# Attention of two batch pairs and a dense block: the second pair interleaved with the first pair's dense layers, row sums as a value column, the Sinkhorn matrix built on chip, s and b applied at the output

The kernel runs on one core of one Trainium2 chip. The metric is the device time of an execution in microseconds; unless said otherwise a time is the median.

## The reference, cut to what matters

```python
# attention: q, k, v are (4, 8, 768, 64), sort_net is (4, 8, 8, 8); 8 blocks of 96 rows
P = sort_net
for _ in range(5):
    P = exp(P - max(P, -1))
    P = P / (sum(P, -1) + 1e-9)
    P = P / (sum(P, -2) + 1e-9)
k_sorted = einsum('bhij,bhjcd->bhicd', P, k_blocks)      # v the same
scores = q_block @ k_sorted_block.T / 8                  # only block i with block i
attn = softmax(scores) @ v_sorted_block
x = attn as (3072 tokens, 512)
# dense block: 512 -> 2048 -> 512
h = x @ w_in
out = (s * relu(h)**2 + b) @ w_out                       # s, b are scalars
```

## The kernel before: the parts that matter

Cuts are marked with `...`. Everything is bf16 on TensorE. A scheduler orders the instructions of each engine by its own model of time, so the order of the source is not the order on the engine.

```python
pd_dram = dramp.tile([NG, 128, 128], BF)                 # zeroed in DRAM first
...                                                      # loads: k, q, v of both pairs, then w_in, w_out
...                                                      # Sinkhorn on sn[32, 8, 8], five rounds
for g in range(NG):                                      # block-diagonal matrix by way of DRAM
    for e in range(2):
        nc.sync.dma_start(out=dst, in_=pT[g * GBH + e * 8: g * GBH + e * 8 + 8])
for g in range(NG):
    nc.sync.dma_start(out=pdg[g], in_=pd_dram[g])
...                                                      # transforms of q, k, v of BOTH pairs
for n in range(L):                                       # up to 5 blocks of 96 tokens
    nc.tensor.matmul(out=pv[0:64, cs], lhsT=VS[:, :, gi_e], rhs=at_e[:, cs], start=True, stop=True)
    nc.tensor.matmul(out=pv[64:128, cs], lhsT=VS[:, :, gi_o], rhs=at_o[:, cs], start=True, stop=True)
    nc.tensor.matmul(out=sm[0:64, cs], lhsT=ones96, rhs=at_e[:, cs], start=True, stop=True)
    nc.tensor.matmul(out=sm[64:128, cs], lhsT=ones96, rhs=at_o[:, cs], start=True, stop=True)
nc.vector.reciprocal(out=smr[:, :W], in_=sm[:, :W])      # row sum repeated over 64 rows of the head
nc.vector.scalar_tensor_tensor(out=XT[:, hp, tok0:tok0 + W], in0=pv[:, :W], scalar=sqrt_s,
                               in1=smr[:, :W], op0=ALU.mult, op1=ALU.mult)
...
# dense block after all attention, 512 tokens at a time
...                                                      # 64 matmuls hps, relu on ACT, square on DVE
for f in range(NF):
    nc.tensor.matmul(out=ops_, lhsT=gt[:, f, m * 128:(m + 1) * 128], rhs=wo[:, f, :],
                     start=(f == 0), stop=False)
nc.tensor.matmul(out=ops_, lhsT=ones_row, rhs=bcs, start=False, stop=True)      # the bias
nc.vector.tensor_copy(out=ot, in_=ops_)
```

The softmax here doesn't subtract the row's maximum and nothing guards it: scores larger than these inputs give would overflow.

## Time and profile before

| | before |
|---|---|
| median, range of 4 runs | 368.1 us, 367.5 to 368.8 |
| profiled span | 366.6 us |
| PE, DVE, ACT, POOL busy | 288.7, 174.0, 120.2, 6.3 us |
| first dense matmul starts | 186.9 us |
| last dense matmul ends | 362.5 us |

The two last lines are from the chain in order of time. The span falls into a front of 187 us, in which loads, DMA waits, transforms and attention follow one another, and a dense part of 176 us in which PE is full. The prediction below shows the lines.

PE is TensorE, DVE VectorE, ACT ScalarE, POOL GpSimd, and PEld TensorE's loads of weights. The granted clock is the share of TensorE's full clock that the profile records. PSUM is the memory that matmuls write to, and to evacuate is to copy a result from there to SBUF. The chain is the work that ended last, followed back from the end of the run.

### The profile page before, as it was taken

The numbers are of one execution on the slowest core, as the hardware profiler recorded it, in microseconds if no ns is written. First come the engines' busy times: TensorE is split into PE (matmuls) and PEld (weight loads), VectorE is DVE, ScalarE is ACT, GpSimd is POOL, SyncE is SP. The second block draws the span as 40 slices with busy tenths as digits, with TensorE's granted clock in tenths as the row PEclk, the third lists the DMA queues.
The fourth block names the chain that finished last, engine by engine and source line by source line (L and its number), as shares of the span: only waits on it lengthen the run. The fifth ranks groups of instructions, "written<-read, shape, count | busy, mean of one in ns | idle before, by whom it ended". The sixth has DMA issues, their size and how long they took to land.

```text
span 366.6 us, 5743 instructions
## 1 busy us (share of the span) xinstructions
PE 288.7 (79%) x2472; PEld 169.9 (46%) x2472; DVE 174.0 (47%) x240; ACT 120.2 (33%) x225; POOL 6.3 (2%) x18
## 2 busy tenths in 40 slices
PE   0070258998666896666499999999999999999995
PEld 0050247987555785555234444444434444434442
DVE  0581250039999819999934124224314414413411
ACT  3100007794323562323036026107206404503600
POOL 6000000000000000000000000000000000000000
PEclk9999999566555555555599999999999999999999
DMA  7999999600000000000000110010010020011011
GB/s 129 217 216 217 215 205 206 107 2 3 2 2 0 2 0 2 0 2 2 1 0 2 57 57 2 29 72 14 30 57 29 3 80 34 2 57 57 2 57 57
DMA packets 8010, 20.42 MB, mean 56 GB/s; under 512 B 1586, under 2 KB 3634, under 8 KB 7218
## 3 DMA queue, kind: packets, MB, share of 16 engines
q0 software_dynamic: 3456, 13.63, 18.6%
q1 hardware_dynamic: 4530, 6.44, 4.9%
q8 instruction: 19, 0.31, 0.3%
q14 instruction: 5, 0.04, 0.0%
HBM read 27.34 MB, written 6.36 MB: 92 GB/s over the span
## 4 chain that ended last, share of the span: by engine, by line
PE 59%; DVE 22%; DMA 12%; ACT 2%; issue 2%; SPq 1%; ACTq 0%
PE hps L257 23%; DVE smr L228 18%; PE ps L174 6%; DMA pd_dram<-pT 5%; DMA pdg<-pd_dram 4%; DMA sn<-in_sort_net_dram 2%; DVE XT L229 2%; PE ps L159 2%; ACT ks L165 2%; PE cs_ps L245 1%; PE ops__3663 L266 1%; PE ops__3642 L266 1%; PE ops__3621 L266 1%; PE ops__3450 L266 1%; PE ops__3429 L266 1%
## 5 line engine op out<-in xcount | busy, mean ns | idle before, releaser
L228 DVE RECIPROCAL smr<-sm 128x480 f32<-128x480 f32 (+1 forms) x32 | 79.5, 2525 | 36.9 <-PE sm L224 36.9
L261 ACT ACTIVATE rt<-hps 128x512 bf16<-128x512 f32 x96 | 57.3, 597 | 113.0 <-PE hps L257 113.0
L257 PE MATMUL hps<-XT,wi 128*128 128x512 bf16 x384 | 83.9, 379 | 0.0
L262 DVE TENSOR_TENSOR gt<-rt 128x512 bf16<-128x512 bf16 x96 | 40.8, 425 | 44.8 <-ACT rt L261 44.8
L257 PEld LDWEIGHTS <-wi 128*128 128x128 bf16 x384 | 37.1, 98 | 45.5 <-issue 1.6
L266 PEld LDWEIGHTS <-gt 128*128 128x128 bf16 x384 | 36.1, 98 | 45.1 <-issue 4.1
L159 PE MATMUL ps<-ident,qb 128*64 128x64 bf16 x384 | 14.5, 241 | 36.5 <-DMA qb<-in_q_dram 34.3
L209 ACT ACTIVATE at_o<-sc_o 96x480 bf16<-96x480 f32 (+1 forms) x32 | 15.6, 487 | 54.6 <-PE pv L218 24.2
L159 PEld LDWEIGHTS <-qb 128*64 128x64 bf16 x384 | 12.1, 153 | 38.8 <-DMA qb<-in_q_dram 34.5
L222 PE MATMUL sm<-at_e,ones 96*64 96x96 bf16 x128 | 21.6, 273 | 9.0 <-DVE smr L228 8.7
L220 PE MATMUL pv<-at_o,vs 96*64 96x96 bf16 x128 | 22.7, 300 | 6.2 <-ACT at_o L209 6.1
L218 PE MATMUL pv<-at_e,vs 96*64 96x96 bf16 x128 | 22.7, 305 | 4.2 <-DVE XT L229 3.5
L165 ACT CAST ks<-ps 128x512 bf16<-128x512 f32 x24 | 12.9, 589 | 37.9 <-PE ps L159 37.8
L201 PE MATMUL sc_o<-qt,ks 64*96 64x96 bf16 x128 | 16.9, 270 | 9.3 <-ACT at_o L209 9.3
L218 PEld LDWEIGHTS <-vs 96*64 96x64 bf16 x128 | 19.3, 199 | 10.0 <-issue 8.8
L174 PE MATMUL ps<-pdg,vb 128*96 128x128 bf16 x128 | 23.6, 347 | 0.4 <-ACT ks L165 0.2
L174 PEld LDWEIGHTS <-vb 128*96 128x96 bf16 x128 | 22.6, 254 | 0.9
L167 DVE CAST qt<-ps 128x512 bf16<-128x512 f32 x24 | 15.5, 687 | 15.6 <-PE ps L159 14.3
L220 PEld LDWEIGHTS <-vs 96*64 96x64 bf16 x128 | 18.7, 203 | 4.3 <-issue 4.2
L176 ACT CAST vs<-ps 96x512 bf16<-96x512 f32 x32 | 18.5, 581 | 5.9 <-PE ps L174 4.5
L224 PE MATMUL sm<-at_o,ones 96*64 96x96 bf16 x128 | 20.2, 276 | 0.0
L201 PEld LDWEIGHTS <-ks 64*96 64x96 bf16 x128 | 12.3, 174 | 12.5 <-issue 10.4
(111 smaller groups left out, 252.4 us busy)
## 6 DMA issues: line engine op xcount, KB each, us to landing
out_dram<-ot SPq DMA_DIRECT2D x24, 256.0 KB, 2.0
kb<-in_k_dram POOLq DMA_DIRECT2D x2, 1536.0 KB, 21.4
qb<-in_q_dram POOLq DMA_DIRECT2D x2, 1536.0 KB, 28.2
vb<-in_v_dram POOLq DMA_DIRECT2D x2, 1536.0 KB, 35.1
wi<-in_moe_w_in_dram POOLq DMA_DIRECT2D x1, 2048.0 KB, 55.2
wo<-in_moe_w_out_dram POOLq DMA_DIRECT2D x1, 2048.0 KB, 64.6
sn<-in_sort_net_dram SPq DMA_DIRECT2D x4, 2.0 KB
pd_dram<-zero SPq DMA_DIRECT2D x2, 32.0 KB, 19.3
```

The source lines that it names most:

```text
L159: nc.tensor.matmul(out=ps[e * 64:(e + 1) * 64, t, :], lhsT=src_t[:, c0 + t, :], rhs=mov[:, e * 64:(e + 1) * 64], start=True, stop=True)
L165: nc.scalar.copy(out=dstt[:, :, c0:c0 + CK], in_=pst)
L174: nc.tensor.matmul(out=ps[:, t, :], lhsT=Vb[:, :, d0 + t], rhs=pdg[g], start=True, stop=True)
L201: nc.tensor.matmul(out=sc_o[:, n * BLK:(n + 1) * BLK], lhsT=KS[64:128, q_idx * NB + i, :], rhs=QT[64:128, q_idx * NB + i, :], start=True, ...
L218: nc.tensor.matmul(out=pv[0:64, cs], lhsT=VS[:, :, gi_e], rhs=at_e[:, cs], start=True, stop=True)
L220: nc.tensor.matmul(out=pv[64:128, cs], lhsT=VS[:, :, gi_o], rhs=at_o[:, cs], start=True, stop=True)
L222: nc.tensor.matmul(out=sm[0:64, cs], lhsT=ones96, rhs=at_e[:, cs], start=True, stop=True)
L228: nc.vector.reciprocal(out=smr[:, :W], in_=sm[:, :W])
L257: nc.tensor.matmul(out=hps, lhsT=wi[:, hp, f * 128:(f + 1) * 128], rhs=XT[:, hp, t0:t0 + TG], start=(hp == 0), stop=(hp == NHP - 1))
L261: nc.scalar.activation(out=rt, in_=hps, func=AF.Relu)
L262: nc.vector.tensor_tensor(out=gt[:, f, :], in0=rt, in1=rt, op=ALU.mult)
L266: nc.tensor.matmul(out=ops_, lhsT=gt[:, f, m * 128:(m + 1) * 128], rhs=wo[:, f, :], start=(f == 0), stop=False)
```

## The change

It has five parts. (1) The Sinkhorn matrix is made on chip: a matmul with a 0/1 matrix spreads the rows of `sn` over partitions, and DVE masks them into block-diagonal form. (2) Loads, transforms and attention of the second batch pair become small pieces, called from slots between the dense matmuls of the first pair. (3) Two columns of ones stand beside the 64 value columns, so that the row sum comes out of the value matmul, one per token, and the reciprocal is taken of 8 numbers. For that the product is turned (tokens on partitions), and PE transposes it back. (4) s and b are applied in the copy of the output; the column sum of w_out comes from Pool and one fp32 matmul. (5) Tiles have 384 tokens, and PSUM is shared by all stages in double banks.

```diff
-    nc.sync.dma_start(out=dst, in_=pT[...])             # and back
+    nc.tensor.matmul(out=pe[:, 0:NB * NB], lhsT=emat[:, g * 128:(g + 1) * 128], rhs=sn..., ...)
+    ...                                                 # eight small DVE operations make pd
-    VSg.append(trs.tile([BLK, D, 128], BF, ...))
+    G.vs = trp.tile([BLK, 128, VW], BF, ...)            # VW = 66
+    nc.gpsimd.memset(G.vs[:, :, D:VW], 1.0)
-    ...                                                 # pv with VS stationary, sm with ones96
-    nc.vector.reciprocal(out=smr[:, :W], in_=sm[:, :W])
+    nc.tensor.matmul(out=pv[0:m, e, n * VW:(n + 1) * VW],
+                     lhsT=atf[:, c0:c0 + m], rhs=G.vs[:, e * 64 + g0 + n, :], ...)
+    nc.vector.reciprocal(out=rec, in_=pvv[:, :, :, D])  # 96 x 8
+    nc.vector.tensor_tensor(out=x..., in0=pvv[:, :, :, 0:D], in1=rec..., op=ALU.mult)
+    nc.tensor.transpose(out=tr..., in_=x..., identity=ident[0:BLK, 0:BLK])
...
+    for p in attention(G0, b2, half): p()               # first pair alone
+    nc.gpsimd.tensor_tensor(out=csum, in0=csum, in1=wo[:, f, :], op=ALU.add)   # 15 adds
+    nc.tensor.matmul(out=bps, lhsT=onesf, rhs=csum, start=True, stop=True)
+    nc.vector.tensor_scalar(out=bias, in0=bps, scalar1=b_bc, ...)
+    raws.append(load_raw(1)); G1, queue = transforms(1); queue += attention(G1, b2, half)
+    ffn1(0, nothing)
+    for t in range(NT):
+        if t + 1 < NT: ...; ffn1(t + 1, slot)           # slot() runs queued pieces
+        ffn2(t, slot)
-    nc.tensor.matmul(out=ops_, lhsT=ones_row, rhs=bcs, start=False, stop=True)
-    nc.vector.tensor_copy(out=ot, in_=ops_)
+    nc.vector.scalar_tensor_tensor(out=ot, in0=ops, scalar=s_bc, in1=bias, op0=ALU.mult, op1=ALU.add)
```

## The prediction

> **What bounds the kernel now.** I read the page's slices first, then the chain that ended last, then the groups by shape, then the stretches. The slices show four phases of 9.2 us slices: loading (to slice 7), transforms, attention on DVE (slices 8 to 19), and a dense stretch with PE at nine tenths.
>
> ```profile
> PE   0070258998666896666499999999999999999995
> DVE  0581250039999819999934124224314414413411
> PEclk9999999566555555555599999999999999999999
> GB/s 129 217 216 217 215 205 206 107 2 3 2 2 0 2 0 2 0 2 2 1 0 2 57 57 2 29 72 14 30 57 29 3 80 34 2 57 57 2 57 57
> ...
> PE 59%; DVE 22%; DMA 12%; ACT 2%; issue 2%; SPq 1%; ACTq 0%
> ```
>
> The chain says that no single engine bounds it: DMA holds the start, DVE the attention, PE the end. In the middle PE is half idle and its granted clock is about half. The chain in order of time gives the two DMA waits and the dense rhythm:
>
> ```profile
> 21.02 20.05 DMA pd_dram<-pT
> 41.13 13.93 DMA pdg<-pd_dram
> ...
> 115.06 4.96 DVE smr L228 x2
> ...
> 186.86 13.92 PE hps L257 x64
> 200.78 3.45 PE ops__2535 L266 x16
> 204.55 3.56 PE ops__2556 L266 x16
> 208.42 3.56 PE ops__2577 L266 x16
> ```
>
> The Sinkhorn matrix is ready at 21 us but goes through DRAM and is back at 55 us, queued behind the bulk loads. Two DVE reciprocals take 4.96 us and the next pair starts 5.84 us later (109.22, 115.06). One dense matmul of 512 columns takes 13.92/64 = 217.5 ns; an output tile starts every 3.87 us, although its 16 matmuls need 3.48, so the seventeenth, the bias matmul, costs 0.39.
>
> The stretches, whose columns are stretch, us, then busy us of PE, PEld, DVE, ACT, POOL, the clock, the DMA share and GB/s, show who is full in attention and in the dense part:
>
> ```profile
> 134.00:182.00 48.00, 29.07 (x372) 23.99 (x373) 46.34 (x32) 13.46 (x32) 0.00 (x0) 0.50 0.00 1
> ...
> 187.00:363.00 176.00, 175.78 (x792) 75.25 (x790) 57.56 (x121) 57.31 (x96) 0.00 (x0) 1.00 0.09 35
> ```
>
> DVE is 97% busy in the first, with clock 0.50; in the second PE is full, and DVE and ACT have two thirds free. These durations are used below:
>
> ```profile
> L228 DVE RECIPROCAL smr<-sm 128x480 f32<-128x480 f32 x16 | 50.4, 3150 | 36.9 <-PE sm L224 36.9
> L229 DVE SCALAR_TENSOR_TENSOR XT<-pv,sqrt_s,smr 128x480 bf16<-128x480 f32 x16 | 9.9, 620 | 0.0
> L167 DVE CAST qt<-ps 128x512 bf16<-128x512 f32 x24 | 15.5, 687 | 15.6 <-PE ps L159 14.3
> L209 ACT ACTIVATE at_o<-sc_o 96x480 bf16<-96x480 f32 x16 | 9.1, 568 | 11.7 <-PE sc_o L201 11.7
> ...
> 60.24 0.93 PE L159 MATMUL ps<-pdg,kb 128*64 128x64 bf16 x32 [0.18 <-ACT ks L165]
> 62.22 1.49 PEld L174 LDWEIGHTS <-vb 128*96 128x96 bf16 x8
> 123.01 2.82 PEld L174 LDWEIGHTS <-vb 128*96 128x96 bf16 x16
> ```
>
> The last three are from the timeline: a q or k transform matmul costs 0.93/32 = 29 ns, and a v transform, whose weights are read with a stride, 1.49/8 = 186 ns at full clock and 2.82/16 = 176 ns at half clock. It is its weight load that sets it, not the clock.
>
> **What the Trainium skill says.** "VectorE: DVE Perf Modes", the walkthrough of the pipeline, says that a reciprocal is an iterative division with a repeat count of 8. The trace agrees in kind: 480 and 288 elements take 3150 and 1900 ns, 6.5 ns each, where 512 plain copies take 692 ns. "TensorE: Matmul & The Clock Gate", Back-to-back issue gap, gives N/2.4 + 2.5 ns: 215.8 ns at 512 against 217.5 here. Its Part 1 says that an idle PE falls to half clock; the attention stretch shows 0.50. "GPSIMD Engine Reference", 3.1 Elementwise, gives 4497 ns for an add of 2048 fp32 elements; the trace before has no such operation, so this stays an estimate: 512 elements in about 1.15 us.
>
> **Part by part.**
>
> *Sinkhorn on chip.* The matrix load is now the first DMA, ahead of the bulk loads. In the trace before, s, sent first, was there within 3 us, so Sinkhorn starts at about 3.5 us instead of 11.6. Five rounds take 1.76 us each (11.65 to 20.4), plus a maximum and a subtraction: done at 13. The expansion by a small matmul and eight DVE operations of some 0.25 us ends at about 16 us, where before it was 55. This removes both DMA waits, 34 us of the chain.
>
> *Loads.* Only q, k, v of the first pair precede the weights. Before, 13.63 MB took from 3.7 to 70.2 us, 0.205 MB/us. Now 4.72 MB land by 25 us, wi by 36, wo (8.9 MB in all) by about 46. The second pair's loads come later, beside PE work.
>
> *Transforms of the first pair.* The instruction order puts the expansion matmul after 22 q matmuls, so PE stops until 14 us. Then 170 q and 192 k at 29 to 33 ns, 11.5 us, and 64 v at 0.18, 11.6 us: done at about 38. Evacuation by DVE (1024 elements, 1.22 us by the slope of the 512 copies) and ACT (1.02) in turn is 0.6 us a piece against 0.93 or 1.45 on PE, so hidden.
>
> *Attention.* The row sum as a value column turns 32 large reciprocals (80.8 us) into 32 of 8 elements (191 ns in Sinkhorn), and drops 256 row-sum matmuls. Per head pair and half batch DVE has 0.2 + 0.7 = 0.9 us, ACT one exponential of 768 columns, 0.80 us (slope 0.83 ns from 400 and 563), PE 8 score matmuls at 40 ns and 8 value matmuls at 60 to 100 ns, 0.8 to 1.1 us. With three double buffers, each held about 1.6 us, two per step, a step takes 1.1 to 1.3 us; four steps and the transposes (16 on PE, a copy of 1536 columns of 1.5 us) make a tile of 5.5 us. Before, one step over eight blocks took 5.84 us; two halves now take about 2.5.
>
> *The bias.* The 16 column-sum matmuls (5.3 us) and 24 bias matmuls (24 x 0.39 = 9.4 us) go away. In their place Pool adds 16 slices of wo: 15 adds at 1.15 = 17 us, with five DMA issues of 0.6 us among them, all after wo lands at 46. The one matmul that uses the sum stands in PE's order right after the first scores of the second tile, and waits for Pool. PE gets there at about 38 + 6 = 44 us; the sum is there at 46 + 17 + 3 = 66. PE works in order, so **22 us are lost here**, which the author probably did not intend. Then three tiles remain, 16.5 us: the dense part starts at about 84 us, against 187 before.
>
> *Dense part.* Tiles of 384 tokens: 512 first-layer matmuls at 384/2.4 + 4.2 = 164 ns, 84 us; 384 second-layer ones at 217.5, 83.5 us. Interleaved on the same PE: 384 transforms at 29 (11 us), 64 v at 180 (11.5), 16 steps at 0.8 (13), 64 transposes at 60 (4): 39.5 us. Some 70 changes between kinds of matmul at about 0.08 us, a guess, add 6. Together 213 us. DVE has 64 squarings of 768 columns at 0.56 (36), 24 output operations at 0.7 (17), evacuations 13 and attention 15, 81 us; ACT 64 x 0.80, evacuations 13 and exponentials 13, 77 us. Both are far below 213, so PE sets it.
>
> *Sum.* 84 + 213 = 297; after the last matmul 366.6 - 362.5 = 4.1 us of copy and DMA stay; the measured time is 1.6 above the profiled span (368.2, 366.6). This makes **302.7**; I round to 300, since my PE costs for attention lean high.
>
> **The rivals.**
> 1. *Pool is quick, or wo lands earlier.* With adds of 0.5 us the sum is ready at 57 us, the stall is 13 us, and the time about 290; with no stall at all 279. For it: Pool's small operations in the trace take 0.2 to 0.28 us for 128 columns. Against it: two inputs, fp32, and the skill's figure. If an add takes 2 us the stall is 35 us, and the time 315.
> 2. *Interleaving stalls PE.* All of hps, scores, values, transposes and transforms share three double buffers, and DVE and ACT serve them in order. A late evacuation then stops dense matmuls too, and a PE that pauses may fall to half clock, as in the attention before. At 0.25 us lost at each of 70 changes, 315 us. Against it: ACT and DVE would be under 40% busy, and a buffer comes round only after two other pieces, some 2.5 us of PE work.
> 3. *The second pair's loads come late.* Their buffers are the first pair's, and they are issued from between the Pool adds, from about 52 us, so 4.72 MB need until about 80. The first q piece stands behind 72 first-layer matmuls, about 84 + 12 = 96 us, v 20 us later. I expect no wait; if Pool takes 2 us an add, v is issued at 80 and still in time.
> 4. *Nothing gained,* because the dense part just grows by what it takes in. It grows by 37 us (176 to 213), yet 103 us vanish in front of it; all but impossible.
>
> **Range and chances.** The uncertain terms are the Pool sum (12 us either way), attention tiles (5), the interleaved work and its changes (10); combined about 16. Range 282 to 317. Even the worst corners of the rivals together, about 335, are 9% faster than 368.2.
>
> **What would show it right or wrong.** Pool should be busy from about 46 to 66 us, and the wait list should show the bias matmul waiting for the last Pool add about 20 us. No large reciprocal remains; the exponentials of 768 columns show 0.80 us. The clock should be 1.0 from the first dense tile to the end. PE's busy share from there should be over 95%. A PE gap inside the dense part, released by an evacuation or by the load of v, would prove rival 2 or 3; a short or missing wait of the bias matmul proves rival 1. The prediction fails most if the interleaved transforms cost PE much more than 29 ns in that company.

## The result, and the profile after

The changed kernel takes **297.6 us** (296.9 to 297.9, 4 runs) against 368.1. The ratio is 0.807, 95% interval 0.806 to 0.809. Here and below ratio and interval are from fast runs; the ratio is not quite that of the medians quoted.

The slices of the changed kernel's page (7.4 us each), and its chain's shares:

```profile
PE   0474982005899999999999999999999999999994
DVE  4763442003473455433533463434354255324221
POOL 8100003993000000000000000000000000000000
PEclk9997555555555999999999999999999999999999
...
PE 71%; ACT 3%; issue 2%; DVE 1%; ACTq 0%
```

The longest wait of PE, from the list of waits (us in total, times, longest):

```profile
PE bps L330 <- POOL csum L328: 22.9, 1, 22.9
```

From 69.5 us to the end the chain is PE almost alone; DVE has gone from 22% to 1%. The shares sum to 77% because the chain, as the profile follows it back, begins with the bias matmul at 69.5 us. What held that matmul is in the list of waits: the Pool adds, and PE's zeros in slices 7 and 8 lie under Pool's nines (third row).

The stretches of the changed kernel, with the columns explained in the prediction: the wait, the rest of the first pair's attention, the dense part.

```profile
46.70:69.50 22.80, 0.00 (x0) 0.00 (x0) 0.00 (x0) 0.81 (x1) 19.89 (x20) 0.50 0.59 112
71.60:91.00 19.40, 16.95 (x234) 14.32 (x232) 13.16 (x27) 10.10 (x12) 0.33 (x1) 0.50 0.45 96
91.00:292.00 201.00, 199.12 (x1652) 114.58 (x1666) 78.95 (x133) 77.41 (x93) 0.00 (x0) 0.99 0.09 31
```

Attention is no longer full on DVE (13.2 of 19.4 us where it had 46.3 of 48.0), and PE is full for 201 us of dense work with everything interleaved. The groups that answer to those of before, by shape:

```profile
L296 DVE TENSOR_TENSOR gt<-rt 128x768 bf16<-128x768 bf16 x64 | 35.6, 556 | 49.6 <-ACT rt L295 49.5
L233 ACT ACTIVATE at<-sc 96x768 bf16<-96x768 f32 x32 | 25.5, 805 | 59.6 <-PE sc L229 59.4
L254 DVE TENSOR_TENSOR x<-pv,rec 96x512 bf16<-96x512 f32 x32 | 22.0, 686 | 1.1
L328 POOL TENSOR_TENSOR csum<-csum,wo 128x512 f32<-128x512 f32 x14 | 16.2, 1156 | 0.8
L253 DVE RECIPROCAL rec<-pv 96x8 f32<-96x8 f32 x32 | 6.4, 201 | 11.2 <-PE pv L248 10.2
```

80.8 us of reciprocals (50.4 for the 16 of 480 elements, 30.4 for the 16 of 288) have become 6.4. The timeline of PE (start, us, what, the number of instructions) gives the marks of the front and the rates in the dense part:

```profile
12.52 1.08 PE L147 MATMUL pe<-sn,emat 32*128 32x64 f32 x4 [2.29 <-DVE identf L101]
28.83 10.75 PE L206 MATMUL tv<-pd,vb 128*96 128x128 bf16 x64 [1.16 <-DMA vb<-in_v_dram]
69.53 2.07 PE L330 MATMUL bps<-csum,onesf 128*128 128x512 f32 x2 [22.91 <-POOL csum L328]
104.69 0.69 PE L196 MATMUL tp<-ident,qb 128*64 128x64 bf16 x32
105.32 1.47 PE L290 MATMUL hps<-xt,wi 128*128 128x384 bf16 x8
161.14 0.38 PE L229 MATMUL sc<-qt,ks 64*96 64x96 bf16 x8
161.45 3.63 PE L304 MATMUL ops<-wo,gt 128*128 128x512 bf16 x15
```

The on-chip matrix is started at 12.5 us, where before its way through DRAM ended at 55. Between dense matmuls 32 transform matmuls take 105.32 - 104.69 = 0.63 us, 20 ns each, and eight score matmuls 0.31 us.

So the dense part starts at 91.0 us instead of 186.9 (95.9 us gained), and lasts to 291.9, which is 200.9 us instead of 175.6 (25.3 lost to the interleaved work): 70.6 us in all, as measured.

### The profile page after: what moved, and what is told of

It is laid out like the page before. It is cut to its first block, busy times and chain, and to the rows that moved or that the text cites. A ratio compares the mean times of both kernels' runs of the same rounds, so it can differ in the third digit from the quotient of the medians.

```text
span 295.9 us, 5457 instructions
## 1 busy us (share of the span) xinstructions
PE 245.7 (83%) x2421; PEld 155.4 (53%) x2438; DVE 117.1 (40%) x220; ACT 104.1 (35%) x126; POOL 27.9 (9%) x42
## 4 chain that ended last, share of the span: by engine, by line
PE 71%; ACT 3%; issue 2%; DVE 1%; ACTq 0%
PE hps L290 28%; PE ops L304 28%; PE tv L206 3%; PE pv L248 3%; PE sc L229 3%; PE tr L265 2%; PE tp L196 2%; ACT at L233 2%; ACT rt L295 1%; PE bps L330 1%; DVE ks L171 0%; DVE ot L307 0%; DVE gt L296 0%; ACT xt L173 0%; ACTq L233 0%
## 5 line engine op out<-in xcount | busy, mean ns | idle before, releaser
L290 PE MATMUL hps<-xt,wi 128*128 128x384 bf16 x512 | 91.5, 330 | 0.5 <-ACT rt L295 0.5
L304 PE MATMUL ops<-wo,gt 128*128 128x512 bf16 x367 | 83.7, 379 | 1.1 <-issue 0.5
L295 ACT ACTIVATE rt<-hps 128x768 bf16<-128x768 f32 x64 | 51.8, 811 | 44.6 <-PE hps L290 42.5
L304 PEld LDWEIGHTS <-gt 128*128 128x128 bf16 x384 | 36.4, 98 | 41.8
L296 DVE TENSOR_TENSOR gt<-rt 128x768 bf16<-128x768 bf16 x64 | 35.6, 556 | 49.6 <-ACT rt L295 49.5
L233 ACT ACTIVATE at<-sc 96x768 bf16<-96x768 f32 x32 | 25.5, 805 | 59.6 <-PE sc L229 59.4
L307 DVE SCALAR_TENSOR_TENSOR ot<-ops,s_bc,bias 128x512 f32<-128x512 f32 x24 | 18.0, 751 | 59.1 <-PE ops L304 59.1
L206 PE MATMUL tv<-pd,vb 128*96 128x128 bf16 x128 | 21.7, 343 | 1.2 <-DMA vb<-in_v_dram 1.2
L206 PEld LDWEIGHTS <-vb 128*96 128x96 bf16 x128 | 21.7, 256 | 1.7 <-DMA vb<-in_v_dram 1.3
L254 DVE TENSOR_TENSOR x<-pv,rec 96x512 bf16<-96x512 f32 x32 | 22.0, 686 | 1.1
L330 PE MATMUL bps<-csum,onesf 128*128 128x512 f32 x2 | 2.1, 1140 | 22.9 <-POOL csum L328 22.9
L248 PE MATMUL pv<-vs,at 96*128 96x66 bf16 (+1 forms) x256 | 17.3, 221 | 2.7 <-ACT at L233 2.6
L328 POOL TENSOR_TENSOR csum<-csum,wo 128x512 f32<-128x512 f32 x14 | 16.2, 1156 | 0.8
L171 DVE CAST vs<-tv 96x1024 bf16<-96x1024 f32 x8 | 9.8, 1221 | 15.9 <-PE tv L206 15.9
L229 PE MATMUL sc<-qt,ks 64*96 64x96 bf16 x256 | 14.7, 249 | 1.1 <-ACT xt L173 0.7
```

The source lines that it names most:

```text
L206: nc.tensor.matmul(out=ps[:, t, :], lhsT=vb[:, :, d0 + t], rhs=pds[g].rearrange("p e m x -> p (e m x)"), start=True, stop=True)
L229: nc.tensor.matmul(out=sc[:, e, n * BLK:(n + 1) * BLK], lhsT=G.ks[pr, g0 + n, :], rhs=G.qt[pr, g0 + n, :], start=True, stop=True)
L233: nc.scalar.activation(out=at, in_=sc[:, :, 0:TG], func=AF.Exp, scale=scale)
L248: nc.tensor.matmul(out=pv[0:m, e, n * VW:(n + 1) * VW], lhsT=atf[:, c0:c0 + m], rhs=G.vs[:, e * 64 + g0 + n, :], start=True, stop=True)
L254: nc.vector.tensor_tensor(out=x[:, :, hp * 128:(hp + 1) * 128].rearrange("p n (e d) -> p e n d", e=2), in0=pvv[:, :, :, 0:D], in1=rec.unsq ...
L290: nc.tensor.matmul(out=hps[:, f, 0:TG], lhsT=wi[:, hp, (f0 + f) * 128:(f0 + f + 1) * 128], rhs=xt[:, hp, :], start=(hp == 0), stop=(hp == ...
```

## The experiments

Besides the changed kernel ten others ran; all but one gave the right result. The kernel before took 368.1 to 368.3 us beside them in every round and on both chips that the record names, so times of different rounds are compared as they are.

| run | what | median us |
|---|---|---|
| changed kernel | | 297.6 |
| e1_sum_late | the bias matmul after the first dense tile | 273.2 |
| e2_sum_on_pe | and the column sum on PE, not Pool | 275.5 |
| e3_no_interleave | changed kernel, second pair before the dense part | 313.4 |
| e4_early_dense | e2, tiles 1 to 3 interleaved as well | 269.1 |
| e5_round_trip | changed kernel, matrix through DRAM | 302.5 |
| e6_round_trip_late | e1, matrix through DRAM | 289.7 |
| e7_bias_matmul | e1, bias by a seventeenth matmul | 283.7 |
| e8_before_copy | kernel before, copy for reciprocal (wrong result) | 347.2 |
| e9_big_recip | e1, reciprocals of 512 elements | 321.3 |
| e10_big_recip_early | e4, reciprocals of 512 elements | 306.2 |

### e1: is the wait for Pool on the path?

```diff
-    bps = psb.tile(...); nc.tensor.matmul(out=bps, lhsT=onesf, rhs=csum, ...)     # before load_raw(1)
     ffn1(0, nothing)
+    bps = psb.tile(...)
+    tc.keep_in_program_order(nc.tensor.matmul(out=bps, lhsT=onesf, rhs=csum, ...))
```

Moving the source line alone changes nothing: in a kernel built that way, but not run, the scheduler puts the matmul back at the same place among PE's instructions (probably because its model has w_out landed long before). It had to be pinned behind the matmul traced before it.

> The one matmul that sums the Pool column sum over partitions is pinned behind the first tile's first-layer matmuls; the Pool adds stay as they are. Theory A (the 22.9 us wait of that matmul for Pool lies on the path): the wait goes and the 2.1 us of the matmul itself, at half clock, shrink to about 1.1: 297.6 - 22.9 - 1.0 = about 274 us, and the attention of tiles 1 to 3 ends at about 66 us instead of 90. Rival B (something else, the second pair's loads or a buffer, ends then and takes the place of the wait): under 10 us gained, 288 or more, with a new PE wait of over 10 us in the list of waits.

Measured: **273.2 us**, 24.4 less than the changed kernel. The stretches of e1:

```profile
39.50:66.00 26.50, 23.02 (x319) 19.22 (x319) 16.20 (x35) 14.94 (x18) 16.50 (x17) 0.50 0.70 125
66.00:267.00 201.00, 200.50 (x1670) 114.53 (x1668) 79.79 (x133) 77.35 (x93) 3.69 (x5) 1.00 0.16 46
```

The four attention tiles now run without a hole beside the Pool adds, and the dense part is as long as before but starts 25 us earlier. Theory A holds and rival B falls: the wait was worth its full length.

### e2: do the Pool adds cost anything else?

```diff
-    nc.gpsimd.tensor_tensor(out=csum, ...)              # 15 adds, and the fp32 matmul
+    for f in range(NF):
+        tc.keep_in_program_order(nc.tensor.matmul(out=bps, lhsT=onesb, rhs=wo[:, f, :], ...))
```

> The column sum on PE: 16 bf16 matmuls of ones with wo, at the same late place; no Pool adds. Theory A: the Pool adds cost nothing once the matmul stands late, so this is e1 plus 16 x 0.2175 - 1.1 = 2.4 us: about 276 us. Rival: the adds slow the loads of the second pair or the other engines; then it is faster than e1 by over 2 us.

Measured: 275.5 us, 2.3 more than e1. That is what the sixteen matmuls were expected to cost (2.4), so the adds cost nothing that these runs can show once nothing waits for them; the only fault was where their reader stood.

### e3: what is the interleaving worth?

```diff
+    run_to(len(queue))                                  # all of the second pair's pieces
+    with tc.issue_after(last[0].ins):                   # dense PE work only behind its last transpose
         ffn1(0, nothing); ...                           # slots empty; xtp bufs 5 -> 8
```

> The changed kernel with its wait for Pool as it is, but the second pair's transforms and attention finished before the first dense matmul (eight token tiles kept instead of five). Interleaved they cost PE 27.7 us in the dense stretch; alone the first pair took 26 us for transforms and about 25 us for four attention tiles, so about 51 us. Theory A (interleaving saves only the PE idle time and half clock of that stage): 297.6 - 27.7 - about 5 of losses at the changes of kind + 51 = about 316 us. Rival (interleaving is the main gain of the change): over 335 us. Rival (interleaving gains nothing as PE is full anyway): within 5 us of 297.6.

Measured: 313.4 us, 15.8 more than the changed kernel. The stretches of e3: transforms of the second pair and the start of its attention, the rest of it, the dense part.

```profile
91.00:118.00 27.00, 24.30 (x519) 22.78 (x519) 14.82 (x17) 14.54 (x15) 0.00 (x0) 0.69 0.01 3
118.00:141.00 23.00, 20.82 (x264) 16.65 (x262) 13.53 (x29) 12.34 (x14) 0.00 (x0) 0.50 0.01 1
141.00:310.00 169.00, 166.53 (x891) 87.43 (x889) 53.74 (x88) 51.84 (x64) 0.00 (x0) 0.99 0.10 38
```

Alone, the second pair takes PE some 48 us, much of it at a granted clock of 0.50; interleaved it lengthens the dense part by 200.9 - 168 = 33 us. The gain is the difference, not the whole stage, because PE has to do this work either way. By the profile PE idles for only 4.9 of the 48.1 us alone (91.0 to 139.1), at a mean clock of 0.61, so most of the gain lies in busy time at the lower clock (43.2 us busy alone, 27.7 interleaved), not in idle time. Theory A holds, both rivals fall.

### e5 and e6: what is the on-chip matrix worth, with the wait and without it?

```diff
-    build_pd(0); build_pd(1)
+    nc.sync.dma_start(out=dst, in_=pT[...]); ...        # zeroed DRAM, write, read back, as before
```

With the round trip come back the four small loads of sort_net; the masks that Pool and DVE built are gone.

> The changed kernel with the Sinkhorn matrix sent through DRAM again, its loads in the order of the changed kernel. If the way back takes the 34 us it took before, the matrix is there at about 47 us instead of 14.5; the k and v transforms end at about 65. The bias matmul now stands before all four attention tiles and its sum is ready at about 69.5 as ever. Theory A (the wait for Pool hides most of the round trip): dense starts at 69.5 + 2 + 25 = 96.5 instead of 91: about 303 us. Rival (the on-chip matrix is worth its 32 us): about 330 us.

> The round trip in the kernel of e1, where the bias matmul no longer waits. Transforms end at about 65, four attention tiles take 25, dense from 90 us: about 297 us, against about 274 for e1. So theory A expects the on-chip matrix to be worth about 23 us here and 5 in e5. Rival: the same worth in both.

Measured: e5 302.5 us, 4.9 more than the changed kernel; e6 289.7, 16.5 more than e1. PE in e5, from its timeline:

```profile
38.05 3.75 PE L182 MATMUL tp<-pd,kb 128*64 128x64 bf16 x159 [15.94 <-DMA pd<-pd_dram]
...
69.40 2.07 PE L314 MATMUL bps<-csum,onesf 128*128 128x512 f32 x2 [12.70 <-POOL csum L312]
```

By e6's chain the round trip ran from 18.5 to 38.0 us, 19.5 us and not the 34 that I took over from the kernel before (matrix at 38 us, not 47), so e6 came out 7 us better than expected. The point stands: PE waits 15.9 us for the matrix in e5, and then 12.7 for the sum (22.9 in the changed kernel), which is ready at 69.4 here and at 69.5 there. A later wait for the same clock time hid most of an earlier part's worth.

### e7: what did the bias matmul cost?

```diff
-                                 rhs=wo[:, f, :], start=(f == 0), stop=(f == NF - 1))
+                                 rhs=wo[:, f, :], start=(f == 0), stop=False)
+            nc.tensor.matmul(out=ops, lhsT=ones_row, rhs=bcs, start=False, stop=True)
+...                                                  # bcs = bias / s, made once; the sum pinned as in e1
-            nc.vector.scalar_tensor_tensor(out=ot, in0=ops, scalar=s_bc, in1=bias, ...)
+            nc.vector.tensor_scalar(out=ot, in0=ops, scalar1=s_bc, scalar2=None, op0=ALU.mult)
```

> The kernel of e1 with the bias added by a seventeenth matmul of one row into each of the 24 output groups again, and s applied alone in the copy. Theory A (a one-row matmul costs PE 0.39 us, as the spacing before said): e1 plus 24 x 0.39 = 9.4, about 283 us. Rival (only its 512 columns count, the rest overlaps): plus 24 x 0.2175 = 5.2, about 279 us. Rival (the copies on DVE were the cost): no change.

Measured: 283.7 us, 10.5 more than e1, which would be 0.44 us for each of the 24. Not all of it is theirs. One of them in the timeline, and the matmul that follows:

```profile
135.02 0.38 PE L306 MATMUL ops<-bcs,ones_row 1*128 1x512 bf16 x1
135.34 0.38 PE L229 MATMUL sc<-qt,ks 64*96 64x96 bf16 x8
```

Here it takes 0.32 us of PE's time; where output tiles follow one another, one starts every 3.88 us (266.01, 269.89), 0.40 more than their sixteen matmuls need. The two profiled runs differ by 11.4 us (spans of 270.7 and 282.1), but 2.3 of these were there before the first one-row matmul: the matmul of the sum starts at 77.2 us in e1 and at 79.5 in e7, since the dense part starts 1.0 us later and its next 60 matmuls take 11.3 us for 10.0. Why is open; the first dense matmuls run at the lower clock for longer in e7. That leaves 9.1 us for the 24, or 0.38 each: a matmul of one row costs PE 1.5 to 1.8 times what its 512 columns do in a row of full ones (0.2175 us). Theory A holds (0.39, 9.4 us in all).

### e8: was the reciprocal the whole bound of the attention before?

```diff
-                    nc.vector.reciprocal(out=smr[:, :W], in_=sm[:, :W])
+                    nc.vector.tensor_copy(out=smr[:, :W], in_=sm[:, :W])
```

> The kernel before with its large reciprocal replaced by a plain copy of the same shape; the result is wrong on purpose. DVE per step falls from 5.84 to about 2.2 us. Theory A (DVE's reciprocal bounds that stage, and PE at half clock with about 3.5 us per step is next): 16 x 2.3 = 37 us less, about 331 us; if PE stays at full clock, about 2.2 us per step and 315 us. Rival (the transforms and loads bound it anyway): over 350 us.

Measured: 347.2 us, only 20.9 less than before, outside both branches of theory A (331 and 315) and short of the rival's (over 350), so neither held as written. The stretch of e8 with the last eight steps:

```profile
125.20:160.00 34.80, 33.03 (x371) 26.73 (x372) 18.42 (x32) 15.39 (x32) 0.00 (x0) 0.50 0.01 2
```

PE is 95% busy at clock 0.50, the chain between 130 and 158 us is PE almost alone, and a step takes 4.3 us (copies of 480 columns at 131.66, 135.97, 140.27). I had read 3.5 us from PE's busy time in the kernel before; but there a part of the score matmuls of the two heads overlapped (one head lies in partitions 0 to 63, the other in 64 to 127), one pair every 80 ns (starts at 122.65, 122.69, 122.73, 122.77 and 122.81 us, the heads in turn). In e8 they ran one head after the other, five in 0.56 us, and scores alone take 44% of that chain. So 16 x (5.84 - 4.3) = 25 us could go at most, and not quite that went. The rival's reason, transforms and loads, is not what the trace shows: the bound passed to PE. Taking the reciprocal away alone is worth 21 us; the changed kernel needed less PE work per step as well (no row-sum matmuls, 1.1 us for a step of half the size).

### e9 and e10: when does a DVE cost matter?

```diff
-            nc.vector.reciprocal(out=rec, in_=pvv[:, :, :, D])
+            nc.vector.reciprocal(out=rec, in_=pvv[:, :, :, D:D + 1].broadcast_to([BLK, 2, HB, D]))
```

> The kernel of e1 with the row sum still a value column, but its reciprocal taken of the sum broadcast to all 512 elements of a step, as large as the values (correct result). By 6.5 ns an element a step costs DVE about 3.35 us instead of 0.2: 32 steps, 101 us more on DVE. Theory A (it costs only where DVE bounds the stage; beside dense matmuls it is hidden): the 16 steps of the first pair become DVE-bound at about 4.1 us instead of 1.55: plus 43 us; the second pair's 50 us fit in DVE's 120 idle us of the dense stretch: plus 0 to 8. About 318 us. Rival (DVE serves in order, so late squarings hold PE up): 340 us or more. Rival (hidden everywhere): under 285.

> The same large reciprocals in the kernel of e4, where three more tiles are interleaved. Theory A: only the first tile pays in full, 4 x 2.6 = 10 us; DVE would be busy 116 + 101 = 217 of some 280 us and come close to the bound in the dense part: plus 5 to 12 there. About 287 us, that is 18 more than e4 where e9 is 45 more than e1. Rival (in-order DVE holds PE up): 310 us or more.

Measured: e9 321.3 us, 48.1 more than e1; e10 306.2, 37.0 more than e4. The reciprocals took 3334 and 3341 ns each, 106 us in all. The stretches of e9 (first pair alone, dense part) and of e10:

```profile
39.50:112.00 72.50, 23.97 (x314) 19.79 (x314) 62.69 (x34) 14.73 (x18) 20.23 (x21) 0.50 0.46 88
112.00:316.00 204.00, 201.82 (x1655) 115.17 (x1674) 125.78 (x134) 77.78 (x93) 0.00 (x0) 0.99 0.08 31
```

```profile
62.00:150.00 88.00, 75.91 (x873) 44.13 (x878) 69.90 (x61) 35.19 (x43) 0.32 (x1) 0.93 0.12 33
150.00:301.00 151.00, 140.63 (x1012) 80.37 (x1024) 101.72 (x97) 51.59 (x63) 0.00 (x0) 0.99 0.09 32
```

In e9 theory A holds: the first pair's stage grows from 26.5 to 72.5 us, and 53 us of reciprocals beside the dense part cost it about 3. In e10 it was too low by 19 us. The waits of PE in e10's whole run:

```profile
PE tr L265 <- DVE x L254: 15.3, 5, 6.2
PE ops L304 <- DVE ot L307: 4.4, 5, 1.8
```

The first tile pays 10.8 us (the first dense matmul starts at 58.7 us instead of 47.9), as expected, and 6.2 of the 15.3 us fall in it. The dense part then takes 241.5 us where e4 needs 215.5, 26 more. PE idles for 21.7 us of it (0.8 in e4), among these 9.1 of transposes waiting for x and 4.4 of output matmuls waiting for their buffer to be copied; some 5 us more are busy time, at a mean clock of 0.96 for 0.99. DVE is not full (70 of 88 us), so what holds PE is not its total. That its chain per tile, four steps of 4 us in order with the squarings, is longer than the slots leave it fits these waits, but no run varies it. The rival named that reason, with a size that was too high. In these runs interleaving hid DVE's cost where its results came in time (e9), and not where PE had to wait for them (e10).

### e4: a kernel that beats both

```diff
-    for b2 in range(GB): ...                            # all four tiles of the first pair
+    for p in attention(G0, 0, 0): p()                   # the first tile only; the rest into the queue
...
-    ffn1(0, nothing)
+    ffn1(0, slot)                                       # and the column sum on PE, pinned, as in e2
```

> The sum on PE as in e2, and the dense part starts after the first attention tile: tiles 1 to 3 of the first pair are interleaved as well. Dense work from about 47 us: 84 + 82.4 for the layers, 27.7 for the second pair, 3 x 3 for tiles 1 to 3 at full clock, 3.5 for the sum, 8 of losses: end of PE at 262, plus 4.1 and 1.7: about 268 us, 8 less than e2. Rival (the layers wait for wi or wo, or for attention tiles that come too late): no faster than e2, with PE waits on DMA or on the exponentials.

Measured: **269.1 us**, 6.4 less than e2 and 28.5 less than the changed kernel (ratio to before 0.730, interval 0.728 to 0.733). PE is busy 51.5 of 53 us from 47 us on and full after that. What is left ahead is 48 us of loads, transforms and one tile.

## Why the prediction was right, and where its sizes were off

| step of the prediction | said | measured |
|---|---|---|
| matrix ready | 16 us | 14.7 |
| v of the first pair landed | 25 | 28.8 |
| first pair's transforms done | 38 | 39.5 |
| Pool add of 512 columns | 1.15 | 1.156 |
| column sum ready | 66 | 69.5 |
| wait of the bias matmul | 22 | 22.9 |
| dense part starts | 84 | 91.0 |
| first layer, second layer on PE | 84, 83.5 | 84.0, 82.4 |
| interleaved PE work | 39.5 | 27.7 |
| changes of kind and small waits | 6 | 7 |
| dense part | 213 | 200.9 |
| tail, and time over span | 4.1 + 1.6 | 4.0 + 1.7 |
| time | 302.7, called 300 | 297.6 |

(The measured PE shares of the dense part are from the chain between 91 and 292 us: 41.8% and 41.0% for the layers, 13.8% for the five interleaved kinds, times 200.9.)

*On-chip matrix.* The mechanism and the times were right. What the prediction did not say is that its worth depends on what waits behind it: 4.9 us in this kernel, 16.5 without the wait for Pool (e5, e6).

*Attention.* Right in kind: DVE is out of the bound, and a PE at half clock with chains through ACT sets it. What was left after the wait took 19.4 us, 6.5 us a tile, where I had 16.5 and 5.5: the step was sized too small, which with the later sum (69.5 for 66, as wo landed at 48.8 and not 46) makes the 7 us by which the dense part starts late. That the bound would pass to PE if only the reciprocal went was not seen in its size (e8).

*The bias.* Right: the wait that takes the place of the matmuls was found in the instruction order before any run, and e1 shows that it costs what it lasts. Its 24 bias matmuls are worth 10.5 us by the medians and 9.1 by the profile, said 9.4 (e7). As built, this part of the change cost 24.4 us to gain these and the 5.3 us of the old column-sum matmuls.

*Dense part.* Too high by 12 us, all of it in one term: interleaved PE work. Between dense matmuls a transform takes 20 ns (said 29), a value transform 151 ns (1.21 us for eight; said 180), a score and value step 0.31 + 0.27 us (said 0.8). I had the rates of stretches that were bound by their evacuation or at half clock. This error and the 7 us late start cancelled in part; the total was nearer than its terms.

*Rivals.* 1 (Pool quick) and 3 (late loads) did not happen; the add took 1.156 us, where the figure of "GPSIMD Engine Reference", 3.1 Elementwise, scaled to 512 elements is 1.12 (I had taken 1.15). 2 (stalls from shared buffers) did not happen either: PE is 99% busy in the dense part, clock 0.99. It is not 1.0 at once, as I had said: the first eleven or so dense matmuls take 0.3 us each, some four microseconds, before they fall to 0.16. e10 shows that rival 2 is real once DVE has twice the work.

The parts do not add up to the gain, since they lie behind one another: interleaving is worth 15.8 us (e3), the missing bias matmuls 10.5 (e7 as measured), the on-chip matrix 4.9, and the new wait costs 24.4. The remainder of some 64 us (70.5 - 15.8 - 10.5 - 4.9 + 24.4 = 63.7) belongs to the new attention step, to smaller loads in front and to their interplay; e8 and e9 show that the reciprocal is a large part of it, but no run splits it cleanly. That stays open.

## What to carry to other kernels

Read the order of each in-order engine, not the source: one cheap matmul whose input comes late stopped PE for 23 us, and pinning it a tile later gave it all back. Interleaving a stage with a PE-bound one is worth what the stage loses by itself to idle time and a lower clock (48 us alone, 33 interleaved), not all of its work; and it stops hiding another engine's cost as soon as PE has to wait for that engine's results. When a part seems to be worth little, look for a later wait that hides it before you call it worthless.

## What the Trainium skill lacked or had wrong

- "VectorE: DVE Perf Modes" names the iterative division of a reciprocal but has no rate for it. Here 480, 512 and 288 fp32 elements from PSUM took 3150, 3334 and 1900 ns, about 6.5 ns each, against 692 ns for a copy of 512.
- "TensorE: Matmul & The Clock Gate", Part 1, does not say what counts as busy. Small matmuls kept PE 95% busy by the profile for 35 us at a granted clock of 0.50 (e8), and 87% for 19 us in the changed kernel; dense 128 x 128 ones brought it to full within some four microseconds (from 91.0 to about 94.7 us in the changed kernel, worked out from its clock of 0.93 between 93 and 105 us).
- The same page, LDWEIGHTS, gives P/1.2 ns for P columns, 80 ns for 96. With columns 128 bytes apart such loads set a pace of 168 to 186 ns (10.75 us for 64 in the changed kernel, at half clock; 1.49 for 8 before, at full clock), about alike at both clocks. Between dense matmuls 64 of them took 11.10 us, 173 ns each, of which PE lost 151, as the first of a group starts to load before the dense matmuls ahead of it give way (133.98 for 134.14 us). "Advanced Engine Details and Errata", SBUF Cachelines, says that such reads are slower, but has no number.
- No page that I read has the cost of a matmul of one row behind full ones: 0.32 to 0.40 us for 512 columns (e7), where a full one takes 0.2175.
